# The second token tile of a gated MLP moved up beside the first, fed from SBUF, and small work exchanged between VectorE and GpSimd

## The chip, the cores and the metric

One core of one Trainium2 chip runs the whole program. The metric is the device time of one execution in microseconds (us). Before the change three executions took 926.74, 927.92 and 930.14 us, median 927.92.

## The reference

Three layers follow one another: attention over keys and values that are averaged in groups of 8, a dense gated MLP on 2304 tokens, and a mixture of 8 experts with one expert per token. The change concerns the end of the first and the beginning of the second.

```python
def _attn_ref(q, k, v):                      # 4 x 8 heads x 576 x 64
    k_p = k.reshape(B, H, Sp, 8, D).mean(axis=3)
    v_p = v.reshape(B, H, Sp, 8, D).mean(axis=3)
    scores = scale * np.matmul(q, k_p.transpose(0, 1, 3, 2))
    scores = scores - np.max(scores, axis=-1, keepdims=True)
    attn = np.exp(scores)
    attn = attn / (np.sum(attn, axis=-1, keepdims=True) + 1e-09)
    return np.matmul(attn, v_p)

def _moe_ref(x, w_gate, w_val, w_out, rms_g):   # 2304 x 512, 512 x 1536, 1536 x 512
    rms = np.sqrt(np.mean(x * x, axis=-1, keepdims=True) + 1e-06)
    xn = x / rms * rms_g
    g = xn @ w_gate
    silu = g * (1.0 / (1.0 + np.exp(-g)))
    val = xn @ w_val
    return silu * val @ w_out

def _moe2_ref(x, w_gate, w1, w2, capacity):     # 8 experts, 512 x 1024 and 1024 x 512
    expert_idx = np.argmax(x @ w_gate, axis=1)
    ...
    h = np.maximum(np.einsum('ecd,edf->ecf', disp, w1), 0.0)
    y = np.einsum('ecf,efd->ecd', h, w2)
    ...
```

## The kernel before

**Split matmuls.** Each f32 operand of a large product is split into a high part and a remainder (`xh`, `xl` and `wgh`, `wgl` and so on), and three products are added in PSUM: high by high, remainder by high, high by remainder. So one product takes three matmuls.

**Attention** runs over 18 row blocks of 128 tokens (block n), each in steps `s0` to `s5`. The first four blocks are done before the MLP starts, the others are strewn among its steps. `s3` gives the unnormalised rows `x0_n` and their sums of squares, `s4` finds 1/rms by an integer seed and three Newton steps of two instructions each (L266 and L267, on GpSimd, on columns of 128x1), `s5a` scales the rows by it on ScalarE, and `s5` transposes them on TensorE. For blocks 0 and 1 `s5` writes the parts `xh`, `xl` of token tile 0 straight into SBUF (L283, L286). For the others it writes to the DRAM buffer `xh_d`, `load_x` (L348) fetches a token tile of two blocks back, and `split_x` (L352 ScalarE, L353 VectorE) makes its parts.

Keys and values are summed in groups of 8 by `pool_sum`: one VectorE reduction (L134), or three GpSimd additions (L136 to L138). For the first batch both used VectorE.

**The MLP** has 9 token tiles of 256 tokens (t) by 12 blocks of the hidden width (j). One such item (t, j) is `g1` (24 matmuls at L365 into a PSUM tile `g`, of which there are two), `tail1` and `tail2` (L371, L372, L376, L378, L379 on ScalarE and VectorE, in program order behind whatever else is queued there), and `g2` (6 matmuls at L404 into `acc`). The PSUM tile of an item is free when L376 has read it.

**Weights** arrive as float64, read as 16-bit pieces, 0.51 MB for each of 36 units (u = 0 to 35: gate, value, output for j = 0, then for j = 1, ...). `conv` turns a unit into f32: a DMA into one of four buffers `cf` (L320, L322), a cast on ScalarE (L329, `cu`), a shift-and-or on VectorE (L332), which frees the buffer, and for gate and value the two parts (L338 ScalarE, L339 GpSimd). `split_o` splits an output weight into `oh`, `ol` (L393 ScalarE, L394 GpSimd). It does so anew for tiles 0 and 1, and once more for tile 2, whose parts then stay for all later tiles.

**Order.** The list `items` says in which order the (t, j) are run. Tiles 0 and 1 are interleaved with tile 1 `SKEW` = 3 blocks behind. From t = 2 on the items follow one another. The attention steps and the loads are tied to positions in this list. A scheduler then orders the instructions of each engine by its own estimate of when each would be ready, and each engine runs its list strictly in order, so an instruction that waits holds up all that stand behind it.

Of the kernel before, what the change touches and what calls it, by code (L numbers as in the profile page):

```python
# [9 lines left out]
F32 = mybir.dt.float32  # L10
F32R = mybir.dt.float32r
# [6 lines left out]
ALU = mybir.AluOpType  # L18
# [4 lines left out]
P = 128  # L23
# [10 lines left out]
NA = 6  # L34
NB1 = 1
NB2 = 7
SKEW = 3
LEAD = 11
NB, H, S, D, SP = 4, 8, 576, 64, 72
DM, NT, NTB = 512, 2304, 18  # L40
FF, NJ, T, NTT = 1536, 12, 256, 9
# [58 lines left out]
class Attention:  # L100
# [152 lines left out]
    def s4(self, n):  # L253
        nc, st, ap = self.nc, self.st[n], self.ap
        am = ap.tile([P, 3], F32, tag="am", name=f"am{n}", bufs=2)
        ri, rt = (ap.tile([P, 1], F32, tag=x, name=f"{x}{n}", bufs=2) for x in ("ri", "rt"))
        ib = ap.tile([P, 1], I32, tag="ib", name=f"ib{n}", bufs=2)
        ss = st.pop("ss")
        nc.vector.tensor_scalar(am[:, 0:1], ss, 1.0 / DM, 1e-6, op0=ALU.mult, op1=ALU.add)
        nc.vector.tensor_scalar(ib, am[:, 0:1].bitcast(I32), 1, None, op0=ALU.logical_shift_right)  # L260
        nc.vector.tensor_scalar(ri.bitcast(I32), ib, -1, RSQRT_SEED, op0=ALU.mult, op1=ALU.add)
        for i in (1, 2):
            nc.vector.tensor_scalar(am[:, i : i + 1], am[:, 0:1], 0.25**i, None, op0=ALU.mult)

        for i in range(3):
            nc.gpsimd.tensor_scalar(rt, ri, ri, am[:, i : i + 1], op0=ALU.mult, op1=ALU.mult)  # L266
            nc.gpsimd.tensor_scalar(ri, rt, -3.0, ri, op0=ALU.add, op1=ALU.mult)  # L267
        st["ri"] = ri

    def s5a(self, n):  # L270
# [3 lines left out]
    def s5(self, n):  # L274
        nc, st = self.nc, self.st.pop(n)
        x0 = st["x0"]
        tp = self.psum(f"xp{n}", n < 4)
        for c in range(4):
            nc.tensor.transpose(tp[:, 128 * c : 128 * c + 128], x0[:, 128 * c : 128 * c + 128], self.ident)
        if n < 2:  # L280
            xh, xl = (x[:, :, 128 * n : 128 * n + 128] for x in self.direct)
            for c in range(4):
                nc.scalar.activation(xh[:, c], tp[:, 128 * c : 128 * c + 128], AF.Copy, scale=self.gT[:, c : c + 1])  # L283
            for c in range(4):
                t = tp[:, 128 * c : 128 * c + 128]
                nc.vector.scalar_tensor_tensor(xl[:, c], t, self.gT[:, c : c + 1], xh[:, c].bitcast(F32), op0=ALU.mult, op1=ALU.subtract)  # L286
            return
        xo = x0.rearrange("p (c m) -> p c m", c=4)
        for c in range(4):
            nc.scalar.activation(xo[:, c], tp[:, 128 * c : 128 * c + 128], AF.Copy, scale=self.gT[:, c : c + 1])  # L290
        for b, s0, m in self.cut(n):
            t0 = b * S + s0
            nc.sync.dma_start(self.xh_d[:, :, t0 : t0 + m.stop - m.start], xo[:, :, m])


class Moe1:
    def __init__(self, tc, wk, wt, pp, xh_d, wg, wv, wo, x1_d, tab_d, out, c, CAP, NS):
        self.tc, self.nc = tc, tc.nc
        self.wk, self.wt, self.pp, self.xh_d, self.c = wk, wt, pp, xh_d, c
        self.src = {"g": wg, "v": wv, "o": wo}  # L300
        self.x1_d, self.tab_d, self.out, self.CAP, self.NS = x1_d, tab_d, out, CAP, NS
        self.W, self.X, self.Hh, self.acc, self.cum = {}, {}, {}, {}, None
        self.G, self.U = {}, {}
        self.L, self.R, self.put = {}, {}, []
        self.O, self.op, self.xt, self.up = {}, None, {}, []

    def wtile(self, nm, j):
        return self.wt.tile([P, 512], F32 if nm == "o" else F32R, tag=f"w{nm}{j}", name=f"w{nm}{j}")
# [73 lines left out]
    def split_o(self, t, j):  # L382

        nc, wk = self.nc, self.wk
        if j in self.O:
            return self.O[j]
        if t < 2:
            oh, ol = (wk.tile([P, 512], F32R, tag=f"o{n}", name=f"o{n}{t}_{j}", bufs=2) for n in "hl")
        else:
            oh = self.wt.tile([P, 512], F32R, tag=f"wo{j - 1}", name=f"oh{j}") if j else self.op.tile([P, 512], F32R, name="oh0")  # L390
            ol = wk.tile([P, 512], F32R, tag="ol", name=f"ol{j}", bufs=2) if j < 2 else self.op.tile([P, 512], F32R, name=f"ol{j}")
            self.O[j] = oh, ol
        nc.scalar.copy(oh, self.W["o", j])  # L393
        nc.gpsimd.tensor_tensor(ol, self.W["o", j], oh.bitcast(F32), op=ALU.subtract)  # L394
        return oh, ol
# [25 lines left out]
    def r1_turn(self, n, x1):  # L421

        nc = self.nc
        tp = self.pp.tile([P, 512], F32, tag="at", name=f"lt{n}")
        for k in range(4):
            nc.tensor.transpose(tp[:, 128 * k : 128 * k + 128], x1[:, 128 * k : 128 * k + 128], self.c["ident"])
        xt = self.wk.tile([P, 512], F32, tag="oh", name=f"xt{n}", bufs=2)
        (nc.vector.tensor_copy if n == NTB - 1 else nc.scalar.copy)(xt, tp)
        self.xt[n] = xt

# [419 lines left out]
def tile_attention_moe_moe(ctx, tc, q, k, v, w_gate, w_val, w_out, rms_g, r_gate, w1, w2, masks, out, *, cap):  # L850
    nc = tc.nc
# [4 lines left out]
    c = mkconsts(tc, cp, r_gate, NS)  # L856
    cnt, cntf = cp.tile([1, 8], I32, name="cnt"), cp.tile([1, 8], F32, name="cntf")
    xh_d = tc.dram_tile([P, 4, NT], F32, name="xh_d")
# [5 lines left out]
    wk = s1.enter_context(tc.tile_pool(name="wk", bufs=1))  # L864
    ld = s1.enter_context(tc.tile_pool(name="ld", bufs=3))
# [14 lines left out]


    stage = [wt.tile([P, 512], F32, tag=f"w{nm}{j}", name=f"st{nm}{j}") for j in range(8, NJ) for nm in ("gh", "gl", "vh", "vl")]
    A = Attention(tc, ap, ld, cv, pp, q, k, v, masks, rms_g, xh_d, c["ident"], M.tile_x(0), stage)


    items = []
# [59 lines left out]
    slot(1, 1)  # L946
    slot(1, 2)
    for i in range(5):
        A.v_pool(0, i, dve=True)
    for i in range(2, LEAD):  # L950
        for z in range(4):
            slot(i, z)
# [7 lines left out]
    for i, (t, j) in enumerate(items[:-1]):  # L960
        st = i + LEAD
        nxt = items[i + 1] if i + 1 < len(items) else None
        if nxt:
            need(max(3 * nxt[1] + NA, unit[0] + NB1))
        slot(st, 0)
        if nxt:
            M.g1(*nxt, 0)
        slot(st, 1)
        if nxt:
            M.g1(*nxt, 1)  # L970
            M.tail1(*nxt)
        slot(st, 2)
        if nxt:
            M.tail2(*nxt)
        M.g2(t, j)
        slot(st, 3)
        for pt in range(1, NTT):
            p0 = pos[pt, 0]
            if i == p0 - 4 - (pt > 1):
                M.load_x(pt)  # L980
            if i in (p0 - 3, p0 - 2):
                M.split_x(pt, i - p0 + 3)
        if unit[0] == 3 * NJ and rp is None and t <= 1 and j == NJ - 1:
            left.close()
            rp = left.enter_context(tc.tile_pool(name="rp", bufs=1, reuse_waits="tile"))
            M.op = rp
            tb = rp.tile([P, E * NCH, 2], F32, name="tb0")
            nc.gpsimd.memset(tb, 0.0)
            nc.gpsimd.memset(tb[:, :, 0:1].bitcast(I32), ZR)
            nc.sync.dma_start(tab[: E * NS, :].rearrange("(p a) t -> p a t", p=P), tb)  # L990
            nc.sync.dma_start(tab[E * NS :, :].rearrange("(p a) t -> p a t", p=P), tb[:, : T0 // P])
            zr = rp.tile([16, 32], F32, name="zr")
            nc.gpsimd.memset(zr, 0.0)
            nc.scalar.dma_start(x1_d[NT : NT + 1, :].rearrange("a (p f) -> (a p) f", p=16), zr)
        if st == end:
            right.close()
            gp = gs.enter_context(tc.tile_pool(name="m2g", bufs=1, side="right", reuse_waits="tile"))
            wr = Weights(nc, w1, w2, gp)
            z = gp.tile([P, DM], F32, name="z")
            nc.gpsimd.memset(z, 0.0)  # L1000
            late = list(range(16))
        if z is not None and late and j % 2 == 0 and P * late[0] < T * t - (T if j < 6 else 0):
            M.zero(late.pop(0), z)
        if t == NTT - 1:
            wr.take(wt, min(32, RN[min(j + 1, NJ - 1)]))
            while nq < min(16, len(wr.parts) // 2):
                wr.split(0, nq, EQ)
                nq += 1
            if j == EJ[0]:
                M.taken()  # L1010
                ey = Early(M, wr)
                ey.gather()
            if j == EJ[1]:
                ey.prep()
        if j == NJ - 1:
            for b, x in enumerate(M.x1out(t)):
                n = 2 * t + b
                s0 = st + 1 + (2 if t == 0 else 3) * b
                at(s0, 0, M.r1_turn, n, x)
                at(s0, 2, M.r1_pe, rp, n, x)  # L1020
                at(s0 + 1, 0, M.r2, rp, n)
                at(s0 + 1, 2, M.r3, n)
                at(s0 + 1, 3, M.r4, n)
# [49 lines left out]
```

## Time and profile before

| | |
|---|---|
| median of three executions | 927.92 us |
| profiled execution | 935.03 us, span of the instructions 933.3 us |
| TensorE matmul busy | 847.3 us, 91% of the span, 5635 instructions |
| VectorE, ScalarE, GpSimd busy | 469.9, 381.6, 289.7 us |
| mean granted TensorE clock | 0.960 of full speed |
| HBM read and written | 78.70 and 18.41 MB |

The page cuts the span into 40 slices of 23.3 us. TensorE is busy in nine tenths or more of nearly all of them. The exceptions are the first five slices, which hold the first attention blocks and the loading of the MLP's weights, and some in the last third, which is the expert layer. A busy TensorE is not one at its peak, since the granted clock may be low, so the two lines are read together. The profiled execution took 7.1 us more than the median.

### The profile page before, as it was taken

The numbers are of one execution on the slowest core, as the hardware profiler recorded it, in microseconds if no ns is written. First come the engines' busy times: TensorE is split into PE (matmuls) and PEld (weight loads), VectorE is DVE, ScalarE is ACT, GpSimd is POOL, SyncE is SP. The second block draws the span as 40 slices with busy tenths as digits, with TensorE's granted clock in tenths as the row PEclk, the third lists the DMA queues.
The fourth block names the chain that finished last, engine by engine and source line by source line (L and its number), as shares of the span: only waits on it lengthen the run. The fifth ranks groups of instructions, "written<-read, shape, count | busy, mean of one in ns | idle before, by whom it ended". The sixth has DMA issues, their size and how long they took to land.

```text
span 933.3 us, 15363 instructions
## 1 busy us (share of the span) xinstructions
PE 847.3 (91%) x5635; PEld 763.6 (82%) x5635; DVE 469.9 (50%) x1323; ACT 381.6 (41%) x881; POOL 289.7 (31%) x397
## 2 busy tenths in 40 slices
PE   5386899999999999998999999999698997799995
PEld 4275799999889999998999999898487985687984
DVE  7986545657564554543343433533436227726243
ACT  3778534545344344331221323321526236625251
POOL 3997435355423020124000003700414113213000
PEclk9678999999999999998999999999799999899997
DMA  9998302221222020032000102314546117727000
GB/s 271 260 281 260 104 24 70 80 79 46 65 85 56 23 69 13 24 103 79 23 23 4 56 6 80 103 46 81 157 160 227 57 50 270 274 92 256 23 24 7
DMA packets 86136, 93.58 MB, mean 100 GB/s; under 512 B 34577, under 2 KB 58129, under 8 KB 86048
## 3 DMA queue, kind: packets, MB, share of 16 engines
q1 hardware_dynamic: 78832, 79.77, 28.4%
q0 software_dynamic: 5984, 12.62, 4.3%
q8 instruction: 53, 0.87, 0.4%
q14 instruction: 35, 0.29, 0.1%
q10 hardware_dynamic: 1232, 0.05, 0.1%
HBM read 78.70 MB, written 18.41 MB: 104 GB/s over the span
## 4 chain that ended last, share of the span: by engine, by line
PE 46%; DMA 23%; issue 16%; POOL 6%; DVE 6%; ACT 2%; another core or an unknown queue 1%; SPq 0%; POOLq 0%; DVEq 0%; ACTq 0%
PE g L365 26%; PE acc L404 12%; DMA xg<-x_d,tb 10%; DMA out_dram<-ys,tb 4%; POOL xg L687 2%; DMA ck<-in_k 2%; DMA cv<-in_v 1%; PE lp L436 1%; PE u L242 1%; DMA tab<-rec,sl 1%; PE s L204 1%; DVE ci L332 1%; DVE ks L134 1%; DMA xl<-xh_d 1%; PE pp L225 1%
## 5 line engine op out<-in xcount | busy, mean ns | idle before, releaser
L365 PE MATMUL g<-xh,wgh 128*128 128x256 f32 x432 | 125.1, 290 | 10.4 <-ACT xh L352 4.3
L365 PE MATMUL g<-xh,wvh 128*128 128x256 f32 x432 | 125.0, 289 | 0.0
L365 PE MATMUL g<-xl,wvh 128*128 128x256 f32 x432 | 124.6, 288 | 0.2 <-issue 0.2
L365 PE MATMUL g<-xh,wvl 128*128 128x256 f32 x432 | 124.4, 288 | 0.0
L365 PE MATMUL g<-xh,wgl 128*128 128x256 f32 x432 | 124.2, 288 | 0.0
L365 PE MATMUL g<-xl,wgh 128*128 128x256 f32 x432 | 124.0, 287 | 0.0
L372 DVE SCALAR_TENSOR_TENSOR u<-u,g 128x256 f32<-128x256 f32 x108 | 45.0, 417 | 105.9 <-ACT u L371 105.1
L365 PEld LDWEIGHTS g<-xh,wgh 128*128 128x128 f32 x432 | 83.0, 192 | 16.0 <-ACT xh L352 5.0
L371 ACT ACTIVATE u<-g 128x256 f32<-128x256 f32 x108 | 41.6, 385 | 126.1 <-PE g L365 102.9
L404 PE MATMUL acc<-oh,hh 128*128 128x512 f32 x216 | 87.5, 409 | 3.4 <-ACT hh L378 3.4
L404 PE MATMUL acc<-ol,hh 128*128 128x512 f32 x216 | 86.5, 401 | 1.6 <-POOL ol L394 1.6
L365 PEld LDWEIGHTS g<-xl,wgh 128*128 128x128 f32 x432 | 83.1, 192 | 3.3
L365 PEld LDWEIGHTS g<-xh,wgl 128*128 128x128 f32 x432 | 83.2, 193 | 2.0
L365 PEld LDWEIGHTS g<-xl,wvh 128*128 128x128 f32 x432 | 83.9, 194 | 0.6 <-issue 0.5
L365 PEld LDWEIGHTS g<-xh,wvh 128*128 128x128 f32 x432 | 84.0, 194 | 0.4 <-issue 0.2
L365 PEld LDWEIGHTS g<-xh,wvl 128*128 128x128 f32 x432 | 83.7, 194 | 0.2
L378 ACT CAST hh<-u 128x256 fp32r<-128x256 f32 x108 | 44.0, 407 | 92.6 <-DVE u L376 91.0
L404 PE MATMUL acc<-oh,hl 128*128 128x512 f32 x216 | 79.4, 403 | 1.8 <-DVE hl L379 1.8
L653 DVE TENSOR_TENSOR r<-a,r 128x512 fp32r<-128x512 f32 x112 | 70.9, 685 | 14.7 <-ACT r L652 13.5
L747 PE MATMUL b<-r,h 128*128 128x512 f32 x288 | 75.1, 397 | 3.4 <-DVE h L739 3.4
L652 ACT CAST r<-a 128x512 fp32r<-128x512 f32 x128 | 72.4, 623 | 13.0 <-PEq L828 5.4
L735 PEld LDWEIGHTS b<-x,r 128*128 128x128 f32 x576 | 74.5, 191 | 3.5
(184 smaller groups left out, 1702.9 us busy)
## 6 DMA issues: line engine op xcount, KB each, us to landing
a<-in_moe_w SPq DMA_DIRECT2D x128, 256.0 KB
cf<-in_moe_w_out SPq DMA_DIRECT2D x12, 511.8 KB
cf<-in_moe_w_gate SPq DMA_DIRECT2D x12, 511.0 KB
cf<-in_moe_w_val SPq DMA_DIRECT2D x12, 511.0 KB
x_d<-x SPq DMA_DIRECT2D x18, 256.0 KB
xl<-xh_d SPq DMA_DIRECT2D x8, 512.0 KB
xh_d<-x SPq DMA_DIRECT2D x14, 256.0 KB
ck<-in_k SPq DMA_DIRECT2D x12, 256.0 KB
```

Of the source, the lines that this page charges most:

```text
L134: nc.vector.tensor_reduce(s[:r], t[:r].rearrange("p (l d) -> p d l", l=8), axis=X, op=ALU.add)
L204: nc.tensor.matmul(s[m, o : o + 144], qs[:, c], self.kT[b][:, mv : mv + 144], start=True, stop=True)
L365: self.nc.tensor.matmul(ps[:, z], a_[:, s], b_[:, c, :], start=(i == 0), stop=(i == 11))
L371: nc.scalar.activation(u, ps[:, 0], AF.Tanh, scale=0.5)
L372: nc.vector.scalar_tensor_tensor(u, u, 1.0, ps[:, 0], op0=ALU.add, op1=ALU.mult)
L378: nc.scalar.copy(hh, u)
L404: self.nc.tensor.matmul(self.acc[t][b], a_[:, s], b_, start=(j == 0 and i == 0), stop=(j == NJ - 1 and i == 2))
L652: nc.scalar.copy(h, s)
L653: (nc.gpsimd if q in gpq else nc.vector).tensor_tensor(l, s, h.bitcast(F32), op=ALU.subtract)
L687: apart(tc, f"xg{x}", GPS.indirect_dma_start(xg[x][:r], None, x1_d, IOA(TB[:r, e * NCH + j, 0:1].bitcast(U32), 0)))
L735: PE.matmul(ps[:, :SB], a_[:, s], b_[:, c], start=(m == 0), stop=(m == 11))
L747: PE.matmul(Y[c], a_, b_, start=(k == 0 and m == 0), stop=(k == 7 and m == 2))
```

## The change

`SKEW` goes from 3 to 1, so the items run (0,0), (0,1), (1,0), (0,2), (1,1), (0,3), (1,2), ... instead of (0,0), (0,1), (0,2), (0,3), (1,0), (0,4), (1,1), ... Blocks 2 and 3 are written straight into SBUF as token tile 1 in the way that blocks 0 and 1 already were, so the two stores of these blocks, the load of tile 1 and its split go. Tile 1 uses the parts of the output weights that tile 0 has made, which are kept in three buffers instead of two. The Newton steps are issued on VectorE, and the five value sums of the first batch are issued as three GpSimd additions each.

```diff
-SKEW = 3
+SKEW = 1
...
         for i in range(3):
-            nc.gpsimd.tensor_scalar(rt, ri, ri, am[:, i : i + 1], op0=ALU.mult, op1=ALU.mult)
-            nc.gpsimd.tensor_scalar(ri, rt, -3.0, ri, op0=ALU.add, op1=ALU.mult)
+            nc.vector.tensor_scalar(rt, ri, ri, am[:, i : i + 1], op0=ALU.mult, op1=ALU.mult)
+            nc.vector.tensor_scalar(ri, rt, -3.0, ri, op0=ALU.add, op1=ALU.mult)
...
-        if n < 2:
-            xh, xl = (x[:, :, 128 * n : 128 * n + 128] for x in self.direct)
+        if n < 4:
+            xh, xl = (x[:, :, 128 * (n % 2) : 128 * (n % 2) + 128] for x in self.direct[n // 2])
...
-        if t < 2:
-            oh, ol = (wk.tile([P, 512], F32R, tag=f"o{n}", name=f"o{n}{t}_{j}", bufs=2) for n in "hl")
+        if t == 1:
+            return self.O2.pop(j)
+        if t == 0:
+            oh, ol = self.O2[j] = tuple(wk.tile([P, 512], F32R, tag=f"o{n}", name=f"o{n}{j}", bufs=SKEW + 2) for n in "hl")
...
-    A = Attention(tc, ap, ld, cv, pp, q, k, v, masks, rms_g, xh_d, c["ident"], M.tile_x(0), stage)
+    A = Attention(tc, ap, ld, cv, pp, q, k, v, masks, rms_g, xh_d, c["ident"], [M.tile_x(t) for t in (0, 1)], stage)
...
-        A.v_pool(0, i, dve=True)
+        A.v_pool(0, i)
...
-        for pt in range(1, NTT):
+        for pt in range(2, NTT):
             p0 = pos[pt, 0]
-            if i == p0 - 4 - (pt > 1):
+            if i == p0 - 5:
                 M.load_x(pt)
```

How this moves the instructions is seen at three places. In the rows, `cf11` is the buffer of unit 11, and `g1_1_0` is the PSUM tile of item (1, 0). The first place is VectorE's list just before the second half of token tile 0 is written (`xl0<-xp1`), which the first MLP matmul needs. Before:

```order
L261 TENSOR_SCALAR ri2_410<-ib2_412 128x1
L332 SCALAR_TENSOR_TENSOR ci13_793<-cf13_790,cu1_523 128x512
L206 TENSOR_REDUCE mx4_964<-s4_0_967 128x4
L207 TENSOR_TENSOR pr4_965<-s4_0_967,mx4_964 128x288
L206 TENSOR_REDUCE mx4_964<-s4_1_991 128x4
L207 TENSOR_TENSOR pr4_965<-s4_1_991,mx4_964 128x288
L332 SCALAR_TENSOR_TENSOR wo4_802<-cf14_799,cu0_521 128x512
L209 TENSOR_REDUCE sm4_966<-pr4_965 128x4
L286 SCALAR_TENSOR_TENSOR xl0_121<-xp1_425,gT_124,xh0_120 128x128 x4
```

The same place after the change:

```order
L332 SCALAR_TENSOR_TENSOR wo3_788<-cf11_785,cu1_541 128x512
L266 TENSOR_SCALAR rt2_423<-ri2_422,am2_421 128x1
L206 TENSOR_REDUCE mx4_946<-s4_0_949 128x4
L267 TENSOR_SCALAR ri2_422<-rt2_423,ri2_422 128x1
L286 SCALAR_TENSOR_TENSOR xl0_121<-xp1_437,gT_126,xh0_120 128x128 x4
```

Units 12, 13 and 14 stood ahead of `xl0<-xp1` and now stand behind it. Ahead of it there are now Newton steps: all twelve of blocks 0 and 1, and four of block 2.

The second place is ScalarE's list around the last weight units. Before:

```order
L371 ACTIVATE u1_0_902<-g1_1_0_877 128x256
L338 CAST wgh11_1795<-ci33_1793 128x512
L329 CAST cu0_521<-cf34_1865 128x512
L290 ACTIVATE x0_4_1121<-xp4_1260,gT_124 128x128 x4
L378 CAST hh1_0_916<-u1_0_902 128x256
L329 CAST cu1_523<-cf35_1874 128x512
L338 CAST wvh11_1870<-ci34_1868 128x512
L208 ACTIVATE pr5_1272<-pr5_1272 128x288
L371 ACTIVATE u0_4_988<-g1_0_4_951 128x256
```

The same place after the change:

```order
L371 ACTIVATE u1_2_1038<-g1_1_2_1007 128x256
L329 CAST cu1_541<-cf33_1900 128x512
L378 CAST hh1_2_1047<-u1_2_1038 128x256
L329 CAST cu0_539<-cf34_1986 128x512
L338 CAST wgh11_1905<-ci33_1903 128x512
L329 CAST cu1_541<-cf35_1995 128x512
L338 CAST wvh11_1991<-ci34_1989 128x512
L371 ACTIVATE u0_4_1116<-g1_0_4_1073 128x256
```

In both the tail of item (0, 4) stands behind the last unit. Before it five tails stood ahead of the last unit, those of (0,0), (0,1), (0,2), (0,3) and (1,0). Now seven do, those of (0,0), (0,1), (1,0), (0,2), (1,1), (0,3) and (1,2).

The third place is ScalarE's list where token tile 2 is split (`xh2<-xl2`), once its load has landed. That load goes into the buffer that tile 0's last `g1`, item (0, 11), reads. Before:

```order
L371 ACTIVATE u0_11_2068<-g1_0_11_2027 128x256
L208 ACTIVATE pr8_1973<-pr8_1973 128x288
L272 ACTIVATE x0_7_1898<-x0_7_1898,ri7_1945 128x512
L393 CAST oh1_8_2162<-wo8_1396 128x512
L378 CAST hh0_11_2085<-u0_11_2068 128x256
L352 CAST xh2_2176<-xl2_2177 128x512 x2
L290 ACTIVATE x0_7_1898<-xp7_2040,gT_124 128x128 x4
L227 COPY pt8_2050<-pp8_0_2051 128x384
L371 ACTIVATE u1_8_2147<-g1_1_8_2109 128x256
```

The same place after the change:

```order
L371 ACTIVATE u0_11_2195<-g1_0_11_2170 128x256
L378 CAST hh0_11_2206<-u0_11_2195 128x256
L155 COPY kt2_2051<-kp2_1_2125 128x128
L352 CAST xh2_2147<-xl2_2148 128x512 x2
L251 ACTIVATE jk8_2107,ss8_2108<-x0_8_2103 128x512
L395 CAST oh1_2569<-wo1_585 128x512
L155 COPY kt2_2051<-kp2_2_2198 128x128
L371 ACTIVATE u1_10_2267<-g1_1_10_2232 128x256
```

Behind the split there stood the tails of items (1, 8) to (1, 11). Now those of (1, 10) and (1, 11) are left.

## Rows read from the trace of the kernel before

**Rows 1.** Windows: start:end, length; PE, PEld, DVE, ACT, POOL busy; clock; DMA share, GB/s.
```profile
30.00:40.00 10.00, 3.48 (x18) 2.10 (x16) 10.00 (x23) 6.91 (x15) 9.84 (x17) 0.80 0.83 237
60.00:100.00 40.00, 31.95 (x208) 28.17 (x207) 26.64 (x47) 28.94 (x58) 30.34 (x33) 0.87 0.87 265
110.00:240.00 130.00, 129.35 (x944) 121.67 (x944) 75.65 (x227) 61.54 (x153) 64.93 (x94) 1.00 0.20 58
```
**Rows 2.** Timeline of TensorE: start, length, instructions [idle before, and what ended it].
```profile
46.70 1.12 PE L279 MATMUL xp<-ident,x 128*128 128x128 f32 x4 [6.37 <-ACT x L272]
...
59.66 0.47 PE L365 MATMUL g<-xh,wgh 128*128 128x256 f32 x1 [2.45 <-DVE xl L286]
...
91.02 0.80 PE L365 MATMUL g<-xh,wgh 128*128 128x256 f32 x2 [4.29 <-ACT xh L352]
...
102.88 0.38 PE L365 MATMUL g<-xh,wgh 128*128 128x256 f32 x1 [3.64 <-DVE u L376]
```
**Rows 3.** The chain that ended last, TensorE and DMA pieces: start, length, what.
```profile
59.66 4.63 PE g L365 x24
...
75.40 6.72 DMA cf<-in_moe_w_val
...
115.52 1.39 PE acc L404 x6
...
119.97 3.47 PE g L365 x29
```
**Rows 4.** VectorE's timeline: conversions (L332) and the second half of tile 0.
```profile
50.68 0.81 DVE L332 SCALAR_TENSOR_TENSOR ci<-cf,cu 128x512 int32<-128x512 int32 x1
...
55.26 2.95 DVE L332 SCALAR_TENSOR_TENSOR wo<-cf,cu 128x512 int32<-128x512 int32 x1
...
58.49 1.11 DVE L286 SCALAR_TENSOR_TENSOR xl<-xp,gT,xh 128x128 fp32r<-128x128 f32 x4
59.89 0.68 DVE L332 SCALAR_TENSOR_TENSOR ci<-cf,cu 128x512 int32<-128x512 int32 x1
...
105.36 0.69 DVE L332 SCALAR_TENSOR_TENSOR wo<-cf,cu 128x512 int32<-128x512 int32 x1
```
**Rows 5.** Instructions of Newton (L266, L267): least, median, most ns; first, last start.
```profile
L266 POOL TENSOR_SCALAR rt<-ri,am x54: 333/345/946, 29.3 to 408.4; 128x1 f32<-128x1 f32 x54
L267 POOL TENSOR_SCALAR ri<-rt,ri x54: 259/268/1219, 31.7 to 408.9; 128x1 f32<-128x1 f32 x54
L260 DVE TENSOR_SCALAR ib<-am x18: 135/153/154, 26.1 to 404.7; 128x1 int32<-128x1 int32 x18
L453 DVE TENSOR_SCALAR ohb<-io,xf x18: 221/231/1005, 197.6 to 635.7; 128x8 bf16<-128x8 f32 x18
```
**Rows 6.** Timelines of VectorE and GpSimd at 213 us.
```profile
213.31 0.67 DVE L453 TENSOR_SCALAR ohb<-io,xf 128x8 bf16<-128x8 f32 x1
212.66 1.29 POOL L394 TENSOR_TENSOR ol<-wo,oh 128x512 fp32r<-128x512 f32 x1 [2.58 <-PE acc L404]
```
**Rows 7.** Busy time of the conversions' own instructions on VectorE and ScalarE, 59 to 105.
```profile
59.00:105.00 46.00, 18.15 (x20) 14.23 (x20) 0.88 0.81 246
```
**Rows 8.** TensorE in 110 to 190: first L365 alone, then L404 alone.
```profile
110.00:190.00 80.00, 51.06 (x370) 47.41 (x370) 1.00 0.19 57
110.00:190.00 80.00, 25.94 (x96) 16.57 (x96) 1.00 0.19 57
```
**Rows 9.** GpSimd's timeline: the value sums of the second batch, first of five.
```profile
19.27 0.73 POOL L136 TENSOR_TENSOR cv<-cv 128x256 f32<-128x256 f32 x1
...
21.00 0.46 POOL L137 TENSOR_TENSOR cv<-cv 128x128 f32<-128x128 f32 x1
21.54 0.32 POOL L138 TENSOR_TENSOR vs<-cv 128x64 f32<-128x64 f32 x1
```
**Rows 10.** Timelines of SP and ScalarE: token tile 2, its load and its split.
```profile
204.48 0.57 SPq L348 DMA_DIRECT2D xl<-xh_d  x1
209.07 1.15 ACT L352 CAST xh<-xl 128x512 fp32r<-128x512 f32 x2 [2.54 <-DMA xl<-xh_d]
```

More of the change, by code (lines that the diff above doesn't have):

```diff
@@ L304, in __init__ @@
         self.L, self.R, self.put = {}, {}, []
-        self.O, self.op, self.xt, self.up = {}, None, {}, []
+        self.O, self.O2, self.op, self.xt, self.up = {}, {}, None, {}, []
     def wtile(self, nm, j):
@@ L386, in split_o @@
             return self.O[j]
-        if t < 2:
-            oh, ol = (wk.tile([P, 512], F32R, tag=f"o{n}", name=f"o{n}{t}_{j}", bufs=2) for n in "hl")
+        if t == 1:
+            return self.O2.pop(j)
+        if t == 0:
+            oh, ol = self.O2[j] = tuple(wk.tile([P, 512], F32R, tag=f"o{n}", name=f"o{n}{j}", bufs=SKEW + 2) for n in "hl")
         else:
             oh = self.wt.tile([P, 512], F32R, tag=f"wo{j - 1}", name=f"oh{j}") if j else self.op.tile([P, 512], F32R, name="oh0")
-            ol = wk.tile([P, 512], F32R, tag="ol", name=f"ol{j}", bufs=2) if j < 2 else self.op.tile([P, 512], F32R, name=f"ol{j}")
+            ol = wk.tile([P, 512], F32R, tag="ol", name=f"ol{j}", bufs=SKEW + 2) if j < 2 else self.op.tile([P, 512], F32R, name=f"ol{j}")
             self.O[j] = oh, ol
@@ L426, in r1_turn @@
             nc.tensor.transpose(tp[:, 128 * k : 128 * k + 128], x1[:, 128 * k : 128 * k + 128], self.c["ident"])
-        xt = self.wk.tile([P, 512], F32, tag="oh", name=f"xt{n}", bufs=2)
+        xt = self.wk.tile([P, 512], F32, tag="oh", name=f"xt{n}", bufs=SKEW + 2)
         (nc.vector.tensor_copy if n == NTB - 1 else nc.scalar.copy)(xt, tp)
```

## The prediction

> **What bounds the kernel now.** I read the busy time by stretch first. From 110 to 240 us TensorE is busy in 129.35 of 130 us at the full granted clock of 2.4 GHz, while VectorE is busy little over half the time [rows 1]. There the kernel is bound by TensorE, and only work that TensorE did earlier can shorten it. From 60 to 100 us it is busy 31.95 of 40 us at a mean clock of 0.87, and from 30 to 40 us 3.48 of 10 [rows 1]. So the change can win something in the first 110 us.
>
> Then I read what TensorE waited for there, in its timeline. The transpose of block 0 waits 6.37 us for the scaled rows, which wait for Newton on GpSimd. The first MLP matmul, at 59.66, waits for the second half of token tile 0. At 91.02 tile 1 begins after a wait of 4.29 us for the split of its load, and at 102.88 item (1, 1) begins after 3.64 us for L376 of item (1, 0), which frees its PSUM tile [rows 2]. The chain of waits shows transfers of weight buffers in this stretch, one of them 6.72 us long [rows 3]. The last conversion of a weight unit starts on VectorE at 105.36 [rows 4].
>
> **The price of an item.** 29 matmuls of `g1` take 3.47 us, so 24 take 2.87. Six of `g2` take 1.39 [rows 3]. From 110 to 190 us there are 370 of the first and 96 of the second [rows 8], which make 44.3 + 22.2 = 66.5 of the 80 us. The other 17% is attention and routing. At the start 24 matmuls took 4.63 us [rows 3], at a mean clock between the two levels of 1.2 and 2.4 GHz.
>
> **Order: the main term.** I compare the points at which the last weight unit stops holding TensorE up. ScalarE and VectorE run in order, and in both kernels the tail of item (0, 4) stands behind all 36 conversions. Before, TensorE has by 102.88 done six `g1` (tile 0's blocks 0 to 4 and (1, 0)) and four `g2`. From then on it hardly waits. After, seven tails stand ahead of the last unit, so with two PSUM tiles nine `g1` and seven `g2` can be done before (0, 5) has to wait for the tail of (0, 4). That is 3 x 2.87 + 3 x 1.39 = 12.8 us of matmuls more. Attention that goes with it is worth 0 to 2.6 us by its share of 17%. I take 1.2, since in TensorE's list it is only block 5's last scores and transposes.
>
> When is the tail of (0, 4) through? Before, units 15 to 35 are converted from 59.89 to 105.36, so 20 units in 45.5 us [rows 4], while the DMA moves 246 GB/s [rows 7]. Two stores of 0.26 MB and a load of 0.51 MB go, at that rate 4.2 us, which would put the last conversion at 101.2. Newton for blocks 2, 3 and 4, 18 instructions, comes onto VectorE in this stretch. VectorE is idle 13.4 of 40 us there [rows 1], which hides most of them, but a conversion behind one of them frees its buffer later. I charge 2 us: 103.2. If the DMA ran at a share of 1 instead of 0.81, the 41.3 us would be 33.5, and the end 93.4. If every one of the 18 took 0.8 us more and nothing hid it, the end would be 115.6. Conversion, L372 and L376 take about 1.3 us more, so item (0, 5) begins at 104.5. The sum: 102.9 - 104.5 + 12.8 + 1.2 = 12.4 us gained.
>
> **Can TensorE be there by then?** That depends on the first MLP matmul. Three conversions (units 12 to 14) are moved behind the second half of tile 0. The first took 0.81 us, the last 2.95 [rows 4], and with a middle one between these they come to 5.6. Sixteen Newton instructions come ahead of it. The trace shows the like of them from both sides: the same kind with constants takes 0.15 us and never more than 0.154, the one with a column as operand 0.23 at the median and up to 1.0 [rows 5]. The latter is the form that Newton has. So 16 cost 2.4 to 16 us. VectorE is full there, 10.00 of 10 us [rows 1], so nothing hides them. Against them stand the wait of 6.37 us for the old Newton chain and the time for which GpSimd, busy 9.84 of 10 us [rows 1], held conversions up. I take 4 us for Newton and 3 us for that relief: 59.7 - 5.6 + 4 - 3 = 55. From 50 to 65 is possible. Nine `g1` and seven `g2` are 35.6 us, with the 17% 42.8, and two `g1` at the lower clock add 3.5, so 101.3. That leaves 3 us for the wait for tile 1's rows of block 3. Both ends meet near 104.5, so neither alone could bring much more.
>
> **The row that speaks against Newton on VectorE.** At 213.31 the instruction with a column operand takes 0.67 us and ends with the GpSimd subtraction that ran from 212.66 to 213.95 [rows 6]. The conversion, which reads two SBUF tiles, takes 0.68 us at 59.89 and 2.95 at 55.26 [rows 4]. The Trainium skill, page "SBUF — State Buffer", section "Who interferes with whom", says that a VectorE instruction with two SBUF inputs and a GpSimd instruction that reads SBUF exclude each other for the whole instruction, and that one with at most one SBUF input does not contend. If a column operand is no second input, Newton costs only 16 x 0.15 = 2.4 us ahead of the first matmul. If it is one, the row at 213.31 holds and Newton is the rival below. The trace agrees with the second reading.
>
> **The smaller edits.** The value sums of the first batch take GpSimd 0.73 + 0.46 + 0.32 = 1.5 us each [rows 9], 7.6 us for five, and VectorE loses five reductions. This lies before 20 us, where block 0's rows are not yet needed: their transpose came at 46.70 [rows 2]. I cost it at 0, with a bound of 1 us either way. Twelve splits of output weights go from ScalarE and GpSimd. Most lay beside a saturated TensorE, so 0. From block 5 on Newton on VectorE lies beside it too, 0, or up to 2 us of scattered waits if tails stand behind it. Tile 2's load now waits for item (0, 11), with only (1, 10) and (1, 11) to cover it: 48 + 12 matmuls and one block's ten attention products, some 9.5 us. It needs 209.07 - 204.48 = 4.6, the split's 1.15 on ScalarE [rows 10] and about as much on VectorE, 6.9. So 0, with up to 4 us if the transfer is late.
>
> After that TensorE's list is the old one shifted, and nothing in the expert layer waits for a point in time that stays. The gain is carried to the end: 935.0 - 12.4 = 922.6 for a profiled execution. That execution stood 7.1 us above the median, so the median becomes 915.5 us.
>
> **Rivals.**
> - Faster still: transfers run closer to full and the first matmul comes at 50. With the last conversion at 98 the gain is 17.6, time 910. With 93.4 and a TensorE that keeps up it is 22, time 906. For it speaks the DMA share of 0.81, against it that the buffers are freed by engines in order.
> - The lock: Newton on VectorE waits out GpSimd's subtractions, the first matmul comes at 62 to 65 and tile 1's rows after 76. TensorE then reaches item (0, 5) at 112 to 114 instead of 104.5. The gain shrinks to 3 to 5 us, time 924. For it speaks the row at 213.31, against it that GpSimd has less to do.
> - Tile 2's load arrives late: 4 us of the gain are lost, time 919.5.
> - Slower: the coupling of conversions and tails. Conversions now stand behind tails of tile 1 on VectorE, these behind TensorE, and TensorE behind conversions by its two PSUM tiles. While one waits, four weight buffers stand idle. If TensorE so stays at the lower clock, an item takes 4.26 x 4.63 / 2.87 = 6.9 us, with attention 8.3. Six items from 72 end at 122, and the last conversion with them. It decides from 115.6 on, where the gain is zero; at 122 the time is 934. For it speaks the wait of 3.64 us of just this kind [rows 2], against it that TensorE has two items per block now, which is slower than the weights arrive.
>
> **How the numbers follow.** The forecast, 909 to 921 us, has a chance of 0.50, the faster rival 0.14, the lock 0.20, the late load 0.08, the slower one 0.08. Half a per cent, 4.6 us, is about what a measurement of this kernel can tell from no change, so the limits are 923.3 and 932.6. Faster: 0.50 + 0.14 + 0.08 and two fifths of the lock, 0.80. Slower 0.07, the rest of the slow rival and three fifths of the lock no change, 0.13. The range of 904 to 926 leaves out a part of the fastest and of the lock's cases and the slow rival.
>
> **What would show it.** Right: the first L365 near 55, item (1, 0) before 76, the last L332 near 103, item (0, 5) near 104.5 with nine `g1` behind it, and no waits of over 1 us for tile 2's split. The lock would show as L266 and L267 on VectorE with a mean well over 0.3 us before 60. The forecast is wrong if the last conversion comes after 110, or if TensorE has idle stretches between 110 and 640 that it did not have.

## The result, and the profile after

The changed kernel takes 915.71 us (median of four, 912.05 to 919.07) against 929.03 us before (four, 926.74 to 932.11). The ratio is 0.985, 95% interval 0.9825 to 0.9875, so about 13 us are gained. The profiled execution took 916.06 us, its span is 914.3.

Busy time by stretch after (the stretches of [rows 1], same columns):

```profile
30.00:40.00 10.00, 5.09 (x21) 3.83 (x19) 10.00 (x23) 6.14 (x14) 8.56 (x11) 0.67 0.78 248
60.00:100.00 40.00, 36.12 (x255) 32.68 (x255) 35.56 (x81) 33.27 (x70) 23.28 (x17) 0.96 0.82 260
110.00:240.00 130.00, 125.41 (x912) 117.14 (x910) 77.45 (x252) 55.98 (x141) 43.92 (x60) 1.00 0.23 63
```

From 60 to 100 us TensorE is busy 36.12 us instead of 31.95, and its mean granted clock is 0.96 instead of 0.87 (1 is 2.4 GHz). From 110 to 240 it is idle 4 us more than before. Up to 110 us, before and then after:

```profile
0.00:110.00 110.00, 71.24 (x400) 59.20 (x401) 85.30 (x163) 70.88 (x151) 77.56 (x115) 0.83 0.87 249
```

```profile
0.00:110.00 110.00, 83.56 (x515) 71.66 (x516) 90.81 (x210) 74.04 (x158) 73.25 (x102) 0.88 0.82 240
```

So TensorE is 115 matmuls ahead by then. From 110 to 240 it loses 32 of them (912 against 944) and from 240 to 400 it wins 33 back (1204 against 1171), so the lead is made before 110 us. TensorE's timeline, the rows that answer to [rows 2] and the later stops:

```profile
43.98 1.11 PE L279 MATMUL xp<-ident,x 128*128 128x128 f32 x4 [3.44 <-ACT x L272]
...
54.10 0.55 PE L365 MATMUL g<-xh,wgh 128*128 128x256 f32 x1
...
68.88 0.40 PE L365 MATMUL g<-xh,wgh 128*128 128x256 f32 x2
...
78.63 0.39 PE L365 MATMUL g<-xh,wgh 128*128 128x256 f32 x1 [1.52 <-DVE u L376]
...
144.60 0.39 PE L365 MATMUL g<-xh,wgh 128*128 128x256 f32 x1 [1.73 <-DVE u L376]
...
237.71 0.50 PE L406 MATMUL acc<-oh,hh 128*128 128x512 f32 x1 [1.71 <-ACT hh L378]
```

The first MLP matmul comes at 54.10 instead of 59.66, and neither the wait of 4.29 us for tile 1's split nor that of 3.64 at 102.88 is there. The conversions and Newton on VectorE, answering to [rows 4, 5] (first the timeline, then the two groups with min/median/max in ns):

```profile
46.39 2.82 DVE L332 SCALAR_TENSOR_TENSOR ci<-cf,cu 128x512 int32<-128x512 int32 x1 [0.49 <-ACT cu L329]
...
99.79 0.68 DVE L332 SCALAR_TENSOR_TENSOR wo<-cf,cu 128x512 int32<-128x512 int32 x1
```

```profile
L266 DVE TENSOR_SCALAR rt<-ri,am x54: 217/269/276, 31.0 to 394.4; 128x1 f32<-128x1 f32 x54
L267 DVE TENSOR_SCALAR ri<-rt,ri x54: 196/207/216, 33.1 to 396.6; 128x1 f32<-128x1 f32 x54
```

The last conversion starts at 99.79 (before 105.36), and no Newton instruction takes over 0.28 us. The two profiled executions differ by 19 us and the medians by 13. Part of the rest is a stretch between 400 and 440 us in which that of before stops and runs at a lower clock, which the changed kernel's lacks (before, then after):

```profile
400.00:440.00 40.00, 37.60 (x250) 34.61 (x249) 16.64 (x85) 11.88 (x32) 15.14 (x20) 0.91 0.33 105
```

```profile
400.00:440.00 40.00, 40.00 (x291) 37.62 (x290) 16.46 (x72) 10.31 (x29) 12.28 (x13) 1.00 0.27 81
```

### The profile page after: what moved, and what is told of

It reads as the page before. It is cut to its first block, busy times and chain, and to the rows that moved or that the text cites. A ratio compares the mean times of both kernels' runs of the same rounds, so it can differ in the third digit from the quotient of the medians.

```text
span 914.3 us, 15327 instructions
## 1 busy us (share of the span) xinstructions
PE 840.4 (92%) x5635; PEld 759.1 (83%) x5635; DVE 480.8 (53%) x1432; ACT 375.0 (41%) x867; POOL 244.1 (27%) x292
## 4 chain that ended last, share of the span: by engine, by line
PE 50%; DMA 22%; issue 16%; DVE 6%; POOL 4%; ACT 2%; POOLq 0%; ACTq 0%; SPq 0%; DVEq 0%
PE g L365 28%; PE acc L406 14%; DMA xg<-x_d,tb 10%; DMA out_dram<-ys,tb 4%; DMA ck<-in_k 2%; POOL xg L689 2%; PE u L242 2%; PE lp L438 1%; DVE ci L332 1%; DMA tab<-rec,sl 1%; PE s L204 1%; DVE ks L134 1%; PE pp L225 1%; ACT cu L329 1%; DMA cv<-in_v 1%
## 5 line engine op out<-in xcount | busy, mean ns | idle before, releaser
L365 PE MATMUL g<-xh,wgh 128*128 128x256 f32 x432 | 124.2, 288 | 3.3 <-DVE u L376 3.2
L365 PE MATMUL g<-xh,wvh 128*128 128x256 f32 x432 | 123.6, 286 | 0.0
L365 PE MATMUL g<-xl,wvh 128*128 128x256 f32 x432 | 123.3, 286 | 0.0
L365 PE MATMUL g<-xl,wgh 128*128 128x256 f32 x432 | 123.1, 285 | 0.0
L365 PE MATMUL g<-xh,wgl 128*128 128x256 f32 x432 | 123.0, 285 | 0.0
L365 PE MATMUL g<-xh,wvl 128*128 128x256 f32 x432 | 122.6, 284 | 0.0
L365 PEld LDWEIGHTS g<-xh,wgh 128*128 128x128 f32 x432 | 82.0, 190 | 8.8 <-DVE u L376 4.2
L365 PEld LDWEIGHTS g<-xl,wgh 128*128 128x128 f32 x432 | 82.0, 190 | 3.5
L365 PEld LDWEIGHTS g<-xh,wgl 128*128 128x128 f32 x432 | 81.9, 190 | 2.0
L365 PEld LDWEIGHTS g<-xh,wvh 128*128 128x128 f32 x432 | 82.5, 191 | 0.2 <-issue 0.2
L365 PEld LDWEIGHTS g<-xh,wvl 128*128 128x128 f32 x432 | 82.6, 191 | 0.1
L365 PEld LDWEIGHTS g<-xl,wvh 128*128 128x128 f32 x432 | 82.5, 191 | 0.0
```

What stands on the lines that cost most here:

```text
L365: self.nc.tensor.matmul(ps[:, z], a_[:, s], b_[:, c, :], start=(i == 0), stop=(i == 11))
```

## The experiments

All kernels are timed against the kernel before on the same chip, whose median was 929.0 to 929.9 us. "g1" counts the matmuls of `g1` that TensorE had started by 110 us, as a measure of how far the stage had come (before: 174). The kernels above 240 take 910 to 920 us, those below take 918 to 934. Each kernel has one trace, of one execution, which can lie some us off the median (6.0 for the kernel before).

| kernel | SKEW | tile 1 fed | Newton | sums | buffers | us | ratio, 95% interval | first L365 | g1 |
|---|---|---|---|---|---|---|---|---|---|
| feed_only | 3 | SBUF | GpSimd | VectorE | 2 | 923.04 | 0.9919 (0.9898 to 0.9941) | 60.6 | 231 |
| newton_only | 3 | DRAM | VectorE | VectorE | 2 | 922.86 | 0.9934 (0.9913 to 0.9954) | 54.2 | 224 |
| skew3_newton_pool | 3 | SBUF | GpSimd | GpSimd | 2 | 924.81 | 0.9947 (0.9925 to 0.9969) | 62.5 | 218 |
| skew3 | 3 | SBUF | VectorE | GpSimd | 2 | 913.40 | 0.9823 (0.9799 to 0.9848) | 54.4 | 248 |
| feed_skew1 | 1 | SBUF | GpSimd | VectorE | 2 | 929.19 | 0.9992 (0.9974 to 1.0011) | 59.9 | 204 |
| no_share | 1 | SBUF | VectorE | GpSimd | 2 | 924.50 | 0.9944 (0.9924 to 0.9964) | 54.5 | 207 |
| no_share_b3 | 1 | SBUF | VectorE | GpSimd | 3 | 916.14 | 0.9854 (0.9827 to 0.9881) | 49.8 | 249 |
| b3_skew2 | 2 | SBUF | VectorE | GpSimd | 3 | 919.76 | 0.9893 (0.9862 to 0.9924) | 54.7 | 244 |
| b3_skew3 | 3 | SBUF | VectorE | GpSimd | 3 | 914.85 | 0.9853 (0.9826 to 0.9880) | 54.9 | 249 |
| changed kernel | 1 | SBUF | VectorE | GpSimd | 3, shared | 915.71 | 0.985 (0.9825 to 0.9875) | 54.1 | 259 |
| newton_pool | 1 | SBUF | GpSimd | GpSimd | 3, shared | 933.94 | 1.0043 (1.0023 to 1.0063) | 68.3 | 186 |
| value_sums_dve | 1 | SBUF | VectorE | VectorE | 3, shared | 918.08 | 0.9865 (0.9836 to 0.9893) | 56.5 | 231 |
| skew3_newton5 | 3 | SBUF | blocks 0 to 4 VectorE | GpSimd | 2 | 909.69 | 0.9815 (0.9780 to 0.9850) | 53.3 | 265 |

Theory at the start: the new order (SKEW) is the gain, as predicted. Rivals: the feed, or Newton's place.

**feed_only.** The kernel before with:

```diff
-        if n < 2:
-            xh, xl = (x[:, :, 128 * n : 128 * n + 128] for x in self.direct)
+        if n < 4:
+            xh, xl = (x[:, :, 128 * (n % 2) : 128 * (n % 2) + 128] for x in self.direct[n // 2])
...
-        for pt in range(1, NTT):
+        for pt in range(2, NTT):
```

> The kernel before with one part of the change: tile 1 is fed without DRAM, SKEW stays 3, Newton stays on GpSimd. Theory (the order is the gain): TensorE still has to stop for the last weight units near 103 to 105 us, so the wait of 4.3 us for tile 1's split only moves into that stop: 927 to 930 us, ratio 0.998 to 1.002. Rival (the feed is the gain, since its wait is gone): 4.3 us less, 924 to 925 us, ratio 0.995.

The gain was 6.9 us, more than the rival's 4.3. TensorE's timeline, with item (1, 0), which began at 91.02 before, and the largest stops after it:

```profile
80.58 0.37 PE L365 MATMUL g<-xh,wgh 128*128 128x256 f32 x1
...
99.09 0.38 PE L365 MATMUL g<-xh,wgh 128*128 128x256 f32 x1 [1.13 <-DVE u L376]
...
105.63 0.39 PE L365 MATMUL g<-xh,wgh 128*128 128x256 f32 x1 [0.55 <-DVE u L376]
```

The stretch before it in the kernel before, by the instructions of L365 alone (TensorE and its weight loads):

```profile
75.00:91.00 16.00, 0.51 (x3) 0.49 (x3) 0.88 0.91 287
```

There `g1` stood still from 75 to 91 us but for three matmuls. Now (1, 0) begins 10.4 us earlier. The row at 105.63 is the 217th of `g1`: nine items are done beside the conversions, whose last starts at 105.50, with SKEW still 3. So the nine items that the prediction counted as the order's gain come with the feed alone.

**feed_skew1.** feed_only with `SKEW = 1`.

> The kernel before with tile 1 fed without DRAM and SKEW = 1; Newton stays on GpSimd, the first value sums on VectorE, both tiles split the output weights themselves. Theory (the order is the gain): most of the 13.3 us comes, 916 to 920 us; the first L365 stays near 59 to 60 us, and what it comes later than in the changed kernel (54.1) is lost of the gain, 0 to 5.6 us. Rival (Newton on VectorE, by the earlier first matmul, is the gain): 925 to 929 us.

The first theory fell here: the gain of the feed is lost again, though the first matmul stays at 59.9 us, and the time is just above the rival's range. TensorE's timeline at block 3's transposes, which complete tile 1, in feed_only and then here:

```profile
76.19 0.60 PE L279 MATMUL xp<-ident,x 128*128 128x128 f32 x4
```

```profile
71.81 0.66 PE L279 MATMUL xp<-ident,x 128*128 128x128 f32 x4 [1.70 <-ACT x L272]
```

With SKEW = 3 the rows are there when TensorE comes to them. With SKEW = 1 it comes to them two items earlier and waits.

**skew3.** The changed kernel with:

```diff
-SKEW = 1
+SKEW = 3
...
-        if t == 1:
-            return self.O2.pop(j)
-        if t == 0:
-            oh, ol = self.O2[j] = tuple(wk.tile([P, 512], F32R, tag=f"o{n}", name=f"o{n}{j}", bufs=SKEW + 2) for n in "hl")
+        if t < 2:
+            oh, ol = (wk.tile([P, 512], F32R, tag=f"o{n}", name=f"o{n}{t}_{j}", bufs=2) for n in "hl")
```

and two buffers for the other users of these tags, as before.

> The changed kernel with SKEW = 3 and without the sharing of output weight parts (both tiles split them, two buffers as before). Theory (the order is the gain): the first L365 stays near 54 us, but TensorE stops later for conversions and the gain is gone, 925 to 930 us. Rival (Newton and the early first matmul are the gain, whatever the order): 916 to 920 us.

The rival holds, by more than it said: with the old order and no sharing the kernel is not slower than the changed one.

**no_share.** The second part of that edit alone, SKEW = 1.

> The changed kernel, but tile 1 splits the output weights again itself (two buffers as before): 12 more ScalarE copies and GpSimd subtractions. Theory (sharing is worth 0, since they lie beside a busy TensorE): 914 to 917 us. Rival (the splits delay conversions and tails before 100 us): 3 to 6 us more than the changed kernel, 919 to 922 us.

8.8 us slower than the changed kernel, more than the rival's 3 to 6. TensorE's timeline between the second and the third item:

```profile
60.26 0.28 PE L365 MATMUL g<-xh,wvl 128*128 128x256 f32 x1
...
63.17 1.77 PE L242 MATMUL u<-v,pt 128*64 128x128 f32 x20 [0.78 <-ACT pt L227]
64.88 0.66 PE L187 MATMUL qp<-ident,qt 128*128 128x128 f32 x4
70.16 1.04 PE L279 MATMUL xp<-ident,x 128*128 128x128 f32 x4 [4.62 <-ACT x L272]
...
75.02 0.40 PE L365 MATMUL g<-xh,wgh 128*128 128x256 f32 x2
```

Item (1, 0) is third here and needs block 3's rows, whose transpose waits 4.62 us for the rows scaled by Newton's result (L272); it begins 14.8 us after the start of the last `g1` of (0, 1). With SKEW = 3, (0, 2) and (0, 3) would be run in that time.

**no_share_b3.** no_share with `bufs=3` in place of `bufs=2`, so only the buffers of sharing, not its saved work.

> no_share (924.5 us) with three buffers in place of two for each half of the output weight parts; both tiles still split them, so no instruction is saved. With three buffers VectorE's list has block 3's Newton ahead of block 4's softmax, with two behind it. Theory (buffers: the missing third buffer changes the lists, and tile 1's rows come late): as the changed kernel, 914 to 918 us, block 3's transposes near 66 instead of 70.2 us. Rival (the twelve splits saved are the gain of sharing): stays at 922 to 926 us.

The buffers theory holds: 916.14 us, as the changed kernel, with all 12 splits done twice. VectorE's list shows what the third buffer changes. Around block 3's Newton (`am3_488`, `ri3_489`) and block 4's softmax (`mx4_954`, `pr4_955`), with two buffers and then with three:

```
L206 TENSOR_REDUCE mx4_954<-s4_0_957 128x4
...
L207 TENSOR_TENSOR pr4_955<-s4_0_957,mx4_954 128x288
L259 TENSOR_SCALAR am3_488<-ss3_486 128x1
L207 TENSOR_TENSOR pr4_955<-s4_1_981,mx4_954 128x288
...
L266 TENSOR_SCALAR rt3_490<-ri3_489,am3_488 128x1
```

```
L259 TENSOR_SCALAR am3_488<-ss3_486 128x1
...
L266 TENSOR_SCALAR rt3_490<-ri3_489,am3_488 128x1
...
L206 TENSOR_REDUCE mx4_954<-s4_0_957 128x4
```

With three, block 3's Newton is ahead, and its transpose starts at 57.39 instead of 70.16. This order is not the whole of it: the changed kernel too has block 4's two L207 first (the second starts at 57.44, block 3's L259 at 59.22), and its transpose still starts at 66.01. The first `g1` is here at 49.80, 4.3 us before the changed kernel's, yet the time is the same; the timeline shows where part of the lead goes:

```profile
101.12 0.38 PE L365 MATMUL g<-xh,wgh 128*128 128x256 f32 x1 [2.06 <-DVE u L376]
```

After nine items TensorE waits for a tail beside the last conversion, which starts at 101.17. That is the other end of the stage.

**skew3_newton_pool.** skew3 with Newton on GpSimd again.

```diff
-            nc.vector.tensor_scalar(rt, ri, ri, am[:, i : i + 1], op0=ALU.mult, op1=ALU.mult)
-            nc.vector.tensor_scalar(ri, rt, -3.0, ri, op0=ALU.add, op1=ALU.mult)
+            nc.gpsimd.tensor_scalar(rt, ri, ri, am[:, i : i + 1], op0=ALU.mult, op1=ALU.mult)
+            nc.gpsimd.tensor_scalar(ri, rt, -3.0, ri, op0=ALU.add, op1=ALU.mult)
```

> skew3 (913.4 us) with Newton back on GpSimd; it differs from feed_only (923.0 us) by the value sums on GpSimd alone. Theory (Newton on VectorE is worth the difference of these two, the value sums nothing): 922 to 925 us, first L365 at 60 us or later. Rival (the value sums on GpSimd relieve VectorE and are the gain): 913 to 916 us.

The theory holds: 11.4 us lost, and no difference from feed_only beyond the intervals, so no gain of the value sums is shown.

**newton_pool.** The same edit on the changed kernel.

> The changed kernel with Newton back on GpSimd. Theory (Newton on VectorE brings the first L365 from 60 to 54 us and tile 1's rows with it, and TensorE has no other stop of this size before 110 us): 921 to 926 us. Rival (what TensorE gains at the start it gives back waiting for conversions): 915 to 918 us.

18.2 us lost, more than expected, and slower than the kernel before. TensorE's timeline:

```profile
49.77 0.36 PE L154 MATMUL kp<-ident,kb 64*128 64x64 f32 x1 [8.99 <-POOL kb L145]
51.20 1.11 PE L279 MATMUL xp<-ident,x 128*128 128x128 f32 x4
...
60.30 0.48 PE L225 MATMUL pp<-ident,pr 128*128 128x128 f32 x1 [5.80 <-ACT pr L208]
...
68.34 0.38 PE L365 MATMUL g<-xh,wgh 128*128 128x256 f32 x1
```

GpSimd's timeline before that:

```profile
42.86 1.28 POOL L339 TENSOR_TENSOR wvl<-ci,wvh 128x512 fp32r<-128x512 f32 x1
44.12 0.78 POOL L266 TENSOR_SCALAR rt<-ri,am 128x1 f32<-128x1 f32 x1
44.86 1.70 POOL L396 TENSOR_TENSOR ol<-wo,oh 128x512 fp32r<-128x512 f32 x1
46.56 1.29 POOL L266 TENSOR_SCALAR rt<-ri,am 128x1 f32<-128x1 f32 x1
47.81 0.32 POOL L138 TENSOR_TENSOR vs<-cv 128x64 f32<-128x64 f32 x1
48.09 1.27 POOL L339 TENSOR_TENSOR wgl<-ci,wgh 128x512 fp32r<-128x512 f32 x1
49.32 0.39 POOL L145 TENSOR_TENSOR kb<-ks,msk 64x128 f32<-64x128 f32 x1
```

GpSimd goes without a pause through subtractions, value sums and Newton, and both of the steps shown stand behind a subtraction. TensorE waits 8.99 us for one key product (L145), with block 0's transposes behind it in its list. Busy time by engine over the first 60 us (GpSimd is the last with a bracket), newton_pool and then the changed kernel:

```profile
0.00:60.00 60.00, 25.78 (x132) 19.52 (x132) 45.12 (x84) 33.72 (x70) 50.04 (x88) 0.77 0.92 266
```

```profile
0.00:60.00 60.00, 37.45 (x194) 30.02 (x195) 49.14 (x120) 36.43 (x79) 45.83 (x79) 0.80 0.95 266
```

**value_sums_dve.** The changed kernel with `A.v_pool(0, i, dve=True)`.

> The changed kernel with the first batch's value sums back on VectorE. Theory (they lie where nobody waits for them): 914 to 918 us. Rival (VectorE, full before 60 us, passes their 1.5 us each on to the first matmul): first L365 at 56 us or later, 918 to 923 us.

Between the two: the first matmul comes at 56.5, as the rival says, but the intervals overlap, so a loss is not shown.

**newton_only.** The kernel before with Newton's two lines on `nc.vector`.

> The kernel before with Newton on VectorE alone; tile 1 still goes through DRAM, SKEW stays 3. Theory (GpSimd is what the first rows wait for before 60 us, and relief there is worth 5 to 6 us with or without the feed): first L365 near 54 us, tile 1's stop for its load ends as much earlier, 922 to 926 us. Rival (without the feed the early start is given back at tile 1's load): 927 to 931 us.

The theory holds: 6.7 us gained without the feed, the first `g1` at 54.23 and (1, 0) at 81.97 instead of 91.02.

**b3_skew3, b3_skew2.** no_share_b3 with `SKEW = 3` and `SKEW = 2`.

> no_share_b3 (916.1 us) with SKEW = 3: no sharing, three buffers, Newton and value sums as in the changed kernel. Theory (with Newton on VectorE the order is worth nothing): 911 to 916 us. Rival (the order as predicted, worth 12 us, only hidden in the other kernels by buffers): 920 us or more.

> no_share_b3 (916.1 us) with SKEW = 2. Theory (the order is worth nothing): 911 to 917 us, between b3_skew3 and no_share_b3. Rival (each step of the order is worth some 6 us): 922 us, in the middle of a rise towards b3_skew3.

With three buffers and all else fixed, SKEW 1, 2 and 3 give 916.1, 919.8 and 914.9 us. 3 and 1 cannot be told apart, and there is no rise from 1 to 3. The 919.8 is above what the theory allowed; it isn't explained.

**skew3_newton5.** skew3 with:

```diff
-            nc.vector.tensor_scalar(rt, ri, ri, am[:, i : i + 1], op0=ALU.mult, op1=ALU.mult)
-            nc.vector.tensor_scalar(ri, rt, -3.0, ri, op0=ALU.add, op1=ALU.mult)
+            E = nc.vector if n < 5 else nc.gpsimd
+            E.tensor_scalar(rt, ri, ri, am[:, i : i + 1], op0=ALU.mult, op1=ALU.mult)
+            E.tensor_scalar(ri, rt, -3.0, ri, op0=ALU.add, op1=ALU.mult)
```

> skew3 (913.4 us) with Newton on VectorE for blocks 0 to 4 only, on GpSimd from block 5 on. Theory (Newton's place matters where GpSimd is full, before 100 us): 911 to 915 us, with the stops for u (L376) after 110 us gone or smaller. Rival (the later blocks matter as much): 917 to 922 us.

909.69 us, the lowest median of all and 1.3 us below the theory's range: the first five blocks' Newton carries the whole gain of Newton's move. What TensorE waited for from 105 to 260 us (in total, times, longest), skew3 and then this kernel, whose lines stand one further down:

```profile
PE acc L404 <- ACT hh L378: 3.9, 3, 1.7
PE g L365 <- DVE u L376: 0.8, 1, 0.8
PE rt L474 <- DVE x L247: 0.6, 1, 0.6
```

```profile
PE acc L405 <- DVE hl L380: 1.0, 1, 1.0
PE xp L280 <- ACT x L273: 0.6, 2, 0.5
PE rt L475 <- DVE x L247: 0.3, 1, 0.3
PE s L204 <- DVE hl L380: 0.3, 1, 0.3
```

The waits fall from 5.3 to 2.2 us. That Newton's later blocks made them is not shown: feed_only, with all of Newton on GpSimd, has 5.0 us of them. The interval (0.978 to 0.985) overlaps that of skew3 and that of the changed kernel (0.9825 to 0.9875), so it beats the kernel before for certain, and the changed one by its median only.

## Why the prediction was right in the time and wrong in the reason

915.5 us was predicted and 915.71 measured, but the mechanism was not the one given. The gain has two sources of about equal size: Newton off GpSimd (6.7 us alone, 11.4 on top of the feed) and the feed of tile 1 (6.9 us alone). The edit that was to bring 12.4 us, the order, brings nothing in any of the three pairs of kernels that differ by it. All of these have the feed; without it the order was not tried.

- **Order, the main term: failed.** It compared six `g1` by 102.88 before with nine by 104.5 after, and gave the three items to SKEW. Before, TensorE had only six because (1, 0), the fifth in its list, could not begin until tile 1's rows had come through DRAM, at 91.02, with (0, 4) behind it. feed_only has nine with SKEW 3. The prediction saw the wait of 4.29 us but did not take it away by itself while keeping the order. And that (0, 5) waits for a tail behind all 36 conversions holds in the changed kernel, where it is the tenth item, but not in feed_only with SKEW 3, where (0, 5) is the eighth and was run, with (1, 2), by 105.63.
- **SKEW = 1 has a price that was not in the sum**: tile 1's rows are wanted two items earlier. In no_share that cost 11.1 us against skew3, in feed_skew1 6.2 us against feed_only. The prediction saw the wait for block 3's rows and left 3 us for it. With three buffers the price cannot be seen (916.1 against 914.9).
- **Newton: wrong sign.** It was charged 4 us before the first matmul and 2 us later, against 3 us of relief. The charge of 4 was right: Newton's instructions on VectorE took 0.27 and 0.21 us, 16 of them some 3.8 us, between the bounds of 2.4 and 16. The relief was the mis-sized term: in newton_pool the first `g1` comes 14.2 us later. Part of this is VectorE's list. The prediction booked the three conversions that move behind tile 0's second half, 5.6 us, beside Newton, but most of such a shift comes with Newton's move: with Newton on GpSimd 15 to 18 conversions start before tile 0's last L286 (15 before the change, 18 in newton_pool), with Newton on VectorE 10 to 13 (13 in newton_only, 12 in the changed kernel). How much of Newton's gain is GpSimd's queue and how much this list is not separated.
- **The lock rival: excluded** for this form. Newton took at most 0.276 us in 108 instructions, 32 of which overlap a GpSimd addition or subtraction by 0.1 us or more. The prediction found that the 0.67 us row of [rows 6] agrees with a column operand that counts as a second SBUF input; for columns of 128x1 these 108 refute that reading. The Trainium skill, page "SBUF — State Buffer", section "Who interferes with whom", says that a VectorE instruction with at most one SBUF input, outside the 2-port modes, does not contend, and that `tensor_scalar` can enter those modes. This agrees with Newton's rows if a column is not counted and they ran outside these modes. The prediction left the condition on the modes out. The instruction at 213.31 is a `TENSOR_SCALAR` too, but 128x8 and not 128x1; whether it ran in such a mode no run here tests, and what held it up is open.
- **First L365 near 55, (1, 0) before 76, last L332 near 103, (0, 5) near 104.5:** 54.10, 68.88, 99.79 and 101.76. Both ends do meet: the changed kernel comes to (0, 5) 2 us after the last conversion starts, and in no_share_b3, 4.3 us earlier at the start, the lead is gone by the tenth item. But the 4.2 us of transfers saved, by which the prediction moved the last conversion, are not seen alone: feed_only saves them too, and its last conversion starts at 105.50, before the change at 105.36.
- **Value sums at 0: no difference is shown.** With Newton on GpSimd (skew3_newton_pool against feed_only) and in the changed kernel (value_sums_dve) the intervals overlap. newton_pool lies above feed_skew1, intervals apart, but it also shares and has three buffers, so the sums' part there is not separated.
- **Sharing at 0: wrong.** Its saved splits show no gain, its third buffer is worth 8.4 us at SKEW 1, and what is seen of it is other lists. At SKEW 3 the third buffer does nothing (914.9 against 913.4). Sharing itself at SKEW 2 or 3 was not tried, since its buffers do not fit in SBUF.
- **Tile 2's load at 0: right.** No stop of TensorE is put down to the split. Scattered waits of up to 2 us beside a busy TensorE came, but that they were Newton's is not shown.

The right sum was luck: two gains that were not seen, of the feed and of Newton, stood against a loss that was not seen, that of SKEW = 1, most of which the third buffer took back. What stays open is how the third buffer brings the scheduler to its better list, and how much each list, rather than the edit itself, decides of the 6 to 11 us at SKEW 1.

## What to carry to other kernels

Where an edit has several parts, take each away in thought alone before the gain is given to one: the wait that the feed removed stood in the profile with its line. A small dependent chain is not priced by its own busy time: in newton_pool the steps shown, some 0.34 us by themselves, stand behind subtractions of 1.28 and 1.70 us. A busy share does not choose the engine either, since before the change VectorE was as full as GpSimd from 30 to 40 us [rows 1]. And where a scheduler makes the lists, a buffer more can move as much as a change of order, so it has to be held fixed in a comparison.

## What the runs showed of the hardware

The conversion at 46.39 in the changed kernel takes 2.82 us where 0.68 is usual. GpSimd's timeline at that time:

```profile
46.18 1.26 POOL L396 TENSOR_TENSOR ol<-wo,oh 128x512 fp32r<-128x512 f32 x1
47.40 1.26 POOL L339 TENSOR_TENSOR wgl<-ci,wgh 128x512 fp32r<-128x512 f32 x1
...
51.17 1.25 POOL L136 TENSOR_TENSOR cv<-cv 104x256 f32<-104x256 f32 x1
```

The two subtractions end at 48.66, and 0.55 us later the conversion does, at 49.21, as if it had run after them. It has two SBUF tiles as inputs, and the rule of the Trainium skill's page "SBUF — State Buffer", section "Who interferes with whom", that such an instruction and one of GpSimd that reads SBUF exclude each other, agrees with it. So VectorE had two kinds of instruction in the same stretch: conversions that can wait GpSimd out, and Newton's that never did. VectorE's timeline has one of them beside the GpSimd addition at 51.17:

```profile
51.76 0.27 DVE L266 TENSOR_SCALAR rt<-ri,am 128x1 f32<-128x1 f32 x1
```

So the price that the lock rival put on Newton's move was not paid.
